# Backward chain cut into sixteen pieces of even TensorE work, and the value projection split around the row sums

## The chip, the cores and the metric

The kernel runs on one core of one Trainium2 chip. The time is the device time of one execution in microseconds (us). The engines are TensorE (PE; its weight loads are listed apart as PEld), VectorE (DVE), ScalarE (ACT), GpSimd (POOL) and SyncE (SP, which only issues transfers; POOL issues some too).

## The reference

The program computes a gated mix of two attention branches over one sequence of 2048 tokens of width 576, and all its gradients:

```
g = sigmoid((x * gate_w).sum(-1))
a = A(x)      # 32 query heads of 18, one shared key and value head, softmax, output projection
b = B(B_x)    # 64 segments of 32 tokens, 32 heads of 128; 8 memory rows stand before each segment
out = g * a + (1 - g) * b
grads = vjp(out)(grad_out)    # of x, wq, wk, wv, wo, mem0, Wq, Wk, Wv, Wo, gate_w
```

In branch B the first eight rows of a segment's output are the memory of the next segment:

```
for s in range(64):
    h = concatenate([mem, xs]); q, k, v = h @ Wq, h @ Wk, h @ Wv     # per head
    o = softmax(mask(q k^T * scale)) v;  o = sum over heads of o @ Wo
    mem = o[:, :8];  outs.append(o[:, 8:])
```

So the forward pass of the memory rows is a chain of 64 dependent segments, and their gradient is a chain of 64 in reverse order. All other work can be done in bulk.

## The kernel before

The memory rows are handled in two chains, `b_chain_fwd` and `b_chain_bwd`. Both are generators: each `yield` ends a piece, and there are sixteen pieces to a segment. Each chain is woven with a sweep of branch A, which is bulk work: `a_pass1` with the forward chain, `a_pass2` with the backward chain. A sweep has 1024 steps and 64 segments have 1024 pieces, so one piece stands against one step. `weave` runs under a manual schedule: what is written first is issued first, on every engine and every queue. The order on TensorE is piece, step, piece, step.

A step n of the backward sweep `a_pass2` issues two matmuls into `b_S` (scores of step n+1), two into two tiles of `b_dP` (step n), one exponential on ScalarE (`b_S` to `b_E`, L1532), two products on VectorE (`b_dP` times `b_E` to `b_dS`, L1553), and four matmuls into `b_acc` (step n-1). `b_S` has one buffer, and `b_dP` has two, one for each of the two tiles, so each waits for the reader of the step before. The forward sweep has the same form with `a_S`, `a_dP`, `a_E`, `a_W` (L1394, L1424), and eight matmuls into `a_acc`. Every fourth step issues two loads on SP (`b_QD`, `b_SD`), eight steps ahead of their use.

A backward segment, by its sixteen pieces (0 to 15):

- 0 to 3: gradient of the segment's memory rows times Wo^T, in two column halves j (tile `r_pj`, 20 matmuls each, five weight blocks of 128 rows, called kts); 12 matmuls, then 8 and a copy to `r_dOm` on ScalarE, twice.
- 4: transpose to `r_dOT` (ScalarE) and the product `r_prod` (VectorE). 5: dP in `r_x`, then `r_dS` (VectorE) and its spread form `r_dSB` (POOL).
- 6, 8, 10: `mem_grad` for v, k and q: 16 matmuls with a full 128x128 array, and a copy to `r_dT` on ScalarE. Piece 6 also has `r_dspad` and `r_dsq` on VectorE. Piece 10 also issues the store of `r_dT` (`dTm_dram`, POOL) and the 14 loads of the next segment (`load`, SP).
- 7, 9, 11 to 14: `heads(wi, hf)`, the gradient times Wv, Wq and Wk (wi 2, 0, 1), in two column halves hf of 288: 32 matmuls each, eight units u of four matmuls side by side. After (1, hf) ScalarE copies the half to `r_hs`. Piece 11 also has `r_xq`: two copies on POOL (`r_xpad`, L828), a transpose on VectorE (L830), four stores on POOL (`pq_dram`, L932). Piece 14 also has `sums` of the first two blocks and `p_blocks` for the next segment (`r_ppad` on POOL, `r_pq` on VectorE, `r_PqB` on POOL).
- 15: the other sums, and the copy to `dm`, which the next segment's piece 0 reads.

In a forward segment, pieces 6 to 9 are: value projection of half 0 (20 matmuls into `c_pj`), scores and exponential (`c_E`), the row sums (two matmuls into `c_x`, L66, and the reciprocal `c_rd`, L359), and value projection of half 1 with the copy `c_v` (L63), the normalised `c_pn` (L365) and its spread form `c_PB` (POOL). Piece 11 (`po`) multiplies `c_PB` by the values.

Of the kernel before, what the change touches and what calls it, by code (L numbers as in the profile page):

```python
# [10 lines left out]
F32 = mybir.dt.float32  # L11
P = 128
# [18 lines left out]
class Kern:  # L31
# [205 lines left out]
    def b_chain_fwd(self, keep, sp, psum):  # L237
        nc = self.nc
        NSEG = self.NSEG
# [47 lines left out]
        for s in range(NSEG):  # L287
            h_ = hm[s % 2]
            nc.gpsimd.dma_start(self.memT_dram[:, :, s, :], h_[:, :, 0:8])
            t2 = {w: sp.tile([P, 8, E], BF16, name=f"c_{w}2", bufs=1) for w in ("k", "q", "v")}  # L290
# [20 lines left out]
            def proj(w, j):  # L311
                pj = self.proj_mem(h_, self.W[w], j, psum, "c_pj", 1)
                self.evac(flat(t2[w], j), pj[:], use="s")
# [38 lines left out]
            Et = sp.tile([P, 2, 64], BF16, name="c_E", bufs=1)  # L352
            nc.scalar.activation(Et[:].rearrange("p a b -> p (a b)"), ps[:], ACT.Exp, scale=SCALEB)
            yield
            den = psum.tile([P, 64], F32, name="c_x", bufs=1)
            self.mm(den[:], lhsT=self.blockones[:], rhs=Et[:, 0, :], start=True, stop=False)
            self.mm(den[:], lhsT=self.blockones[:], rhs=Et[:, 1, :], start=False, stop=True)
            rd = sp.tile([P, 64], F32, name="c_rd", bufs=1)
            nc.vector.reciprocal(rd[:], den[:])  # L359
            yield  # L360
            proj("v", 1)
            if s + 1 < NSEG:
                kx = load_k(s + 1)
            pn = sp.tile([P, 2, 64], BF16, name="c_pn", bufs=1)
# [21 lines left out]
            if s + 1 < NSEG:  # L386
# [21 lines left out]
                hs = None  # L408
                pm = None
                for lo, hi in ((0, 256), (256, 512), (512, 576), (576, 576)):  # L410
                    if hi > lo:
                        ph = half(lo, hi)
                    if lo:
                        kts = range(lo // P - 2, min(lo // P, NKT)) if lo < 576 else (4,)
# [5 lines left out]
                    if hi > lo:  # L420
                        hs = sp.tile([P, 256], F32, name="c_hs", bufs=1)
# [371 lines left out]
    def b_chain_bwd(self, keep, sp, psum):  # L793
        nc = self.nc
        NSEG = self.NSEG
# [37 lines left out]
        def p_blocks(pT):  # L833
            pq = to_q((pT[:, 1, :],), "p", nc.gpsimd)
            B = sp.tile([P, 8, 4, 8], BF16, name="r_PqB", bufs=1)
            self.expand(B[:], pq[:, 0, :, 0:8], 8)
            return B

        nxt = load(NSEG - 1)
        PqB = p_blocks(nxt["pT"])  # L840
        for s in reversed(range(NSEG)):
            L = nxt
            d_ = dm[s % 2]
            pT = L["pT"]
            nc.gpsimd.dma_start(self.dmT_dram[:, :, s, :], d_[:, :, 0:8])
            dOm = sp.tile([P, 8, E], BF16, name="r_dOm", bufs=1)
            for j in range(2):
                pj = psum.tile([P, 512], F32, name="r_pj", bufs=2)
                for kts in ((0, 1, 2), (3, 4)):
                    self.proj_part(pj, d_, self.WoT, j, kts)  # L850
                    if s == NSEG - 1 and j == 0 and kts[0] == 3:
                        self.load_WT()
                    if kts[0] == 3:
                        self.evac(dOm[:, 4 * j:4 * j + 4, :].rearrange("p u e -> p (u e)"), pj[:], use="s")
                    yield
            src = self.mem_T(dOm, psum, "r_x", 1)
            dOT = sp.tile([P, 8, 4, 8], BF16, name="r_dOT", bufs=1)
            nc.scalar.copy(dOT[:], src)
            prod = sp.tile([P, 8, 4, 8], BF16, name="r_prod", bufs=1)
            nc.vector.tensor_tensor(out=prod[:].rearrange("p u c q -> p (u c q)"),  # L860
                                    in0=dOT[:].rearrange("p u c q -> p (u c q)"), in1=L["oT"][:], op=ALU.mult)
            for c in range(4):
                nc.gpsimd.dma_start(self.mtok["dO"][s * 8:(s + 1) * 8, c * 1024:(c + 1) * 1024], self.m_rows(dOm, c))
            yield
            pd = psum.tile([P, 2, 64], F32, name="r_x", bufs=1)
            self.mm(pd[:].rearrange("p a b -> p (a b)"), lhsT=self.zeros[:], rhs=self.zeros[:], start=True, stop=False)
            for u in range(8):
                for c in range(4):
                    self.mm(pd[32 * c:32 * c + 32, 0, 8 * u:8 * u + 8], lhsT=L["vxT"][:, 8 * c + u, :],
                            rhs=dOT[:, u, c, :], start=False, stop=False, tp=(0, 32 * c))  # L870
            for u in range(8):
                for c in range(4):
                    self.mm(pd[32 * c:32 * c + 8, 1, 8 * u:8 * u + 8], lhsT=L["vmT"][:, 8 * c + u, :],
                            rhs=dOT[:, u, c, :], start=False, stop=False, tp=(0, 32 * c))
            for rg in range(2):
                for c in range(4):
                    self.mm(pd[32 * c:32 * c + 32, rg, :], lhsT=self.negones[:, 0:32], rhs=prod[:, :, c, :],
                            start=False, stop=True, tp=(0, 32 * c))
            dS = sp.tile([P, 2, 64], BF16, name="r_dS", bufs=1)
            nc.vector.scalar_tensor_tensor(out=dS[:], in0=pd[:], scalar=SCALEB, in1=pT[:], op0=ALU.mult, op1=ALU.mult)  # L880
            dSB = sp.tile([P, 16, 4, 8], BF16, name="r_dSB", bufs=1)
            self.expand(dSB[:], dS[:].rearrange("p a (u q) -> p (a u) q", q=8), 16)
            yield
            dT = sp.tile([P, 3, 8, 32], BF16, name="r_dT", bufs=1)
            hs = sp.tile([P, D], F32, name="r_hs", bufs=1)
            ph = {}

            def heads(wi, hf):
                if hf not in ph:
                    ph[hf] = psum.tile([P, 288], F32, name="r_pj", bufs=2)  # L890
                for u in range(8):
                    for g in range(4):
                        self.mm(ph[hf][32 * g:32 * g + 32, :], lhsT=dT[:, wi, u, :],
                                rhs=self.WT[wi][:, 8 * g + u, 288 * hf:288 * hf + 288],
                                start=(wi == 2 and u == 0), stop=(wi == 1 and u == 7), tp=(0, 32 * g))
                if wi == 1:
                    nc.scalar.copy(hs[:, 288 * hf:288 * hf + 288], ph[hf][:])

            def sums(kts):
                for kt in kts:  # L900
                    ncols = KT_ROWS[kt]
                    self.mm(pm[0:ncols, kt, :], lhsT=hs[:, kt * P:kt * P + ncols], rhs=self.selF[:, :])

            def mem_grad(wi, name, pairs):
                pg = psum.tile([P, 8, 32], F32, name=name, bufs=2 if name == "r_pj" else 1)
                for u in range(8):
                    for n, (l, r) in enumerate(pairs):
                        self.mm(pg[:, u, :], lhsT=l[u], rhs=r[u], start=(n == 0), stop=(n == 1))
                nc.scalar.copy(dT[:, wi], pg[:])

            rows = lambda t, lo=0: [t[:, u, lo:lo + E] for u in range(8)]
            blk = lambda t, u0=0: [f(t[:, u0 + u]) for u in range(8)]
            mem_grad(2, "r_pj", ((rows(mrow["dx"], E), [seln] * 8), (rows(dOm), blk(PqB))))
            dSq = to_q((dS[:, 1, :],), "ds", nc.vector)
            yield
            heads(2, 0)
            yield
            mem_grad(0, "r_x", ((rows(L["kx"]), blk(dSB)), (rows(mrow["k"]), blk(dSB, 8))))
            dSqB = sp.tile([P, 8, 4, 8], BF16, name="r_dSqB", bufs=1)
            self.expand(dSqB[:], dSq[:, 0, :, 0:8], 8)  # L920
            yield
            heads(2, 1)
            yield
            mem_grad(1, "r_x", ((rows(mrow["dx"]), [seln] * 8), (rows(mrow["q"]), blk(dSqB))))
            nc.gpsimd.dma_start(self.dTm_dram[s // 16][:, :, s % 16, :], dT[:].rearrange("p w u c -> p w (u c)"))
            if s:
                nxt = load(s - 1)
            yield
            heads(0, 0)
            xq = to_q((pT[:, 0, :], dS[:, 0, :]), "x", nc.gpsimd)  # L930
            for c in range(4):
                nc.gpsimd.dma_start(self.pq_dram[s // 4, s % 4, :, c, :, 32 * (s % 4):32 * (s % 4) + 32],  # L932
                                    xq[32 * c:32 * c + 8].rearrange("p i u k -> p (i u) k"))
            yield
            heads(0, 1)
            yield
            heads(1, 0)
            yield
            heads(1, 1)
            pm = psum.tile([P, NKT, 8], F32, name="r_x", bufs=1)  # L940
            sums((0, 1))
            if s:
                PqB = p_blocks(nxt["pT"])
            yield
            sums((2, 3, 4))
            dn = dm[1 - s % 2]
            nc.vector.tensor_copy(dn[:, 0:4, 0:8], pm[:, 0:4, :])
            nc.vector.tensor_copy(dn[0:64, 4, 0:8], pm[0:64, 4, :])
            yield
# [849 lines left out]
```

## Time and profile before

| what | value |
|---|---|
| median of 3 runs | 6491.99 us (6484.06 to 6493.47) |
| the profiled execution | 6472.94 us, span of its core 6471.1 us, mean granted TensorE clock 0.971 |
| PE busy | 5931.5 us, 92% of the span |
| DVE, ACT, POOL busy | 3769.7 (58%), 3481.2 (54%), 1952.8 us (30%) |
| forward weave | from about 507 to 2436 us |
| backward weave | from about 3251 to 5039 us |

A busy share is an average over the whole span. The times of the two weaves are those of their first and last exponential in the timeline. A wait in the profile names the engine or transfer that came last; PE's matmuls are pipelined, so start times show more than ends.

### The profile page before, as it was taken

To read this page: it belongs to the slowest core of one execution; us is meant where nothing else is said; L and a number is where in the kernel's file an instruction comes from. 1 tells how busy PE (TensorE), PEld (TensorE's weight loads), DVE (VectorE), ACT (ScalarE), POOL (GpSimd) and SP (SyncE) were. 2 spreads that over 40 slices of the span, in tenths; PEclk is the share of its full clock that TensorE was granted. 3 is DMA by queue.
4 is the path that set the end of the run, shared out by engine and by line. 5 is a ranking of instruction groups with operands and counts; after the bars stand their busy time and mean duration, and the time that the engine had idled before them with its cause. 6 is when DMAs were issued, how large, how long until landed. Compare 5 with 4: busy or idle time off the path is not lost. (4 is left out here: it accounts for less than half of the span.)

```text
span 6471.1 us, 208564 instructions
## 1 busy us (share of the span) xinstructions
PE 5931.5 (92%) x88611; PEld 3332.0 (51%) x88822; DVE 3769.7 (58%) x7061; ACT 3481.2 (54%) x5105; POOL 1952.8 (30%) x3451
## 2 busy tenths in 40 slices
PE   7898999999999995999879999999999899899997
PEld 5443444444444443778634444444444677675443
DVE  5336777777777773666568888888887211111111
ACT  3326777777777773656556767667776322211100
POOL 3002333333333333444423333333333111112212
PEclk9998999999999997999989999999999899999998
DMA  4636666666664435999854443333434799896643
GB/s 152 225 145 114 115 120 119 120 117 118 120 118 104 98 79 167 252 253 263 251 184 101 103 102 102 97 100 102 102 102 100 201 247 245 232 275 213 216 146 111
DMA packets 1368108, 991.94 MB, mean 153 GB/s; under 512 B 931613, under 2 KB 1184806, under 8 KB 1356486
## 3 DMA queue, kind: packets, MB, share of 16 engines
q1 hardware_dynamic: 1285030, 780.53, 49.3%
q0 software_dynamic: 82144, 198.05, 9.6%
q8 instruction: 696, 11.40, 0.7%
q14 instruction: 238, 1.95, 0.1%
HBM read 552.41 MB, written 384.76 MB: 145 GB/s over the span
## 5 line engine op out<-in xcount | busy, mean ns | idle before, releaser
L1424 DVE TENSOR_TENSOR a_W<-a_dP,a_E 128x512 bf16<-128x512 f32 x2048 | 1314.8, 684 | 478.9 <-PE a_dP L66 377.0
L1553 DVE TENSOR_TENSOR b_dS<-b_dP,b_E 128x512 bf16<-128x512 f32 x2048 | 1315.8, 684 | 328.0 <-PE b_dP L66 245.4
L1532 ACT ACTIVATE b_E<-b_S 128x1024 bf16<-128x1024 f32 x1024 | 1048.9, 1024 | 529.2 <-PE b_dP L66 393.6
L1394 ACT ACTIVATE a_E<-a_S 128x1024 bf16<-128x1024 f32 x1024 | 1052.1, 1027 | 134.5 <-PE a_dP L66 120.9
L66 PE MATMUL b_dP<-b_KV,b_QD 32*128 32x512 bf16 x2048 | 584.9, 382 | 5.2 <-DVE b_dS L1553 5.2
L66 PE MATMUL b_S<-b_KV,b_QD 32*128 32x512 bf16 x2048 | 401.6, 385 | 128.9 <-ACT b_E L1532 82.4
L66 PE MATMUL a_dP<-a_QD,l_KV 32*128 32x512 bf16 x2048 | 513.3, 382 | 1.0 <-DVE a_W L1424 0.8
L66 PE MATMUL w_acc<-w_d,w_h 128*128 128x512 bf16 (+1 forms) x2352 | 470.9, 379 | 2.5
L66 PE MATMUL a_S<-a_QD,l_KV 32*128 32x512 bf16 x2048 | 399.6, 383 | 74.3 <-ACT a_E L1394 72.4
L66 PE MATMUL r_pj<-WT,r_dT 128*32 128x288 bf16 x12288 | 447.0, 288 | 0.0
L66 PE MATMUL a_acc<-a_W,l_WK 128*32 128x512 bf16 x4096 | 410.5, 390 | 0.1
L66 PE MATMUL b_acc<-b_dS,b_SD 128*32 128x512 bf16 x2048 | 406.0, 393 | 0.0
L66 PE MATMUL b_acc<-b_E,b_SD 128*32 128x512 bf16 x2048 | 405.8, 393 | 0.0
L66 PE MATMUL a_acc<-a_E,l_VK 128*32 128x512 bf16 x4096 | 399.9, 380 | 0.0
L66 PEld LDWEIGHTS <-r_dT 128*32 128x32 bf16 x12288 | 330.6, 97 | 78.9 <-issue 1.1
L1027 DVE COPY y_T<-y_pt 128x512 bf16<-128x512 bf16 x256 | 96.8, 419 | 461.1 <-PE y_pt L71 443.6
L66 PEld LDWEIGHTS <-w_h 128*128 128x128 bf16 (+1 forms) x2400 | 213.1, 100 | 244.5 <-issue 3.4
L66 PEld LDWEIGHTS <-hm 128*32 128x32 bf16 x7680 | 207.0, 97 | 229.2 <-issue 15.0
L66 PEld LDWEIGHTS <-b_SD 128*32 128x32 bf16 x4096 | 105.3, 93 | 421.3 <-issue 420.3
L66 PEld LDWEIGHTS <-b_QD 32*128 32x128 bf16 x4096 | 142.9, 91 | 327.2 <-issue 245.3
L66 PEld LDWEIGHTS <-l_WK 128*32 128x32 bf16 x4096 | 105.3, 93 | 349.0 <-issue 348.9
L1013 ACT CAST y_tdk<-y_pk 128x512 bf16<-128x512 f32 x128 | 75.1, 587 | 379.9 <-PE y_pk L66 240.8
(410 smaller groups left out, 11558.8 us busy)
## 6 DMA issues: line engine op xcount, KB each, us to landing
b_QD<-qd_dram SPq DMA_DIRECT2D x256, 128.0 KB
b_SD<-sd_dram SPq DMA_DIRECT2D x256, 128.0 KB
dOx_dram<-p_tok SPq DMA_DIRECT2D x16, 1024.0 KB
c_vx<-vx_dram SPq DMA_DIRECT2D x256, 64.0 KB
krow_dram<-c_k POOLq DMA_DIRECT2D x64, 256.0 KB, 2.6
qrow_dram<-c_q POOLq DMA_DIRECT2D x64, 256.0 KB, 2.8
vrow_dram<-c_v POOLq DMA_DIRECT2D x64, 256.0 KB, 4.5
x_q<-qx_dram SPq DMA_DIRECT2D x32, 512.0 KB
```

The costliest lines, as they stand in the source:

```text
L66: return self.nc.tensor.matmul(out, lhsT, rhs, start=start, stop=stop, tile_position=tp, skip_group_check=True)
L1013: nc.scalar.copy(d[w][:, r, :], pk[:])
L1027: nc.vector.tensor_copy(T_[t][w][:], pt[:])
L1394: nc.scalar.activation(E_[n][:], S.pop(n)[:], ACT.Exp, scale=SCALEA)
L1424: nc.vector.tensor_tensor(out=W_[n][:, i, :], in0=dP[i][:], in1=E_[n][:, i, :], op=ALU.mult)
L1532: nc.scalar.activation(E_[n][:], S.pop(n)[:], ACT.Exp, scale=SCALEA)
L1553: nc.vector.tensor_tensor(out=D_[n][:, i, :], in0=dP[i][:], in1=E_[n][:, i, :], op=ALU.mult)
```

## The change

The forward chain issues 12 of the 20 matmuls of the second half of the value projection in the piece of the row sums' place, ahead of them, and the row sums, their reciprocal, the last 8 matmuls and the rest of the old projection piece in the next one. The backward chain's Wo^T projection takes three pieces instead of four (16, 12 and 12 matmuls), across the border of the column halves. The 48 units of `heads` are taken from one list, six or three at a time, so that a piece may end in the middle of a weight or of a column half: six in each pure piece, three behind the second and third `mem_grad`. Both chains still have sixteen pieces to a segment. In the new numbering a backward segment has the projection in 0 to 2, `r_dOT` in 3, dP in 4, `mem_grad` in 5, 7 and 9, units in 6 to 14, `r_xq` in 11, the copy of the first half of `r_hs` in 12, `p_blocks` in 13, the first sums in 14, the others in 15. The same instructions are issued, in another order.

```diff
@@ b_chain_fwd
             nc.scalar.activation(Et[:].rearrange("p a b -> p (a b)"), ps[:], ACT.Exp, scale=SCALEB)
             yield
+            pj = psum.tile([P, 512], F32, name="c_pj", bufs=1)
+            self.proj_part(pj, h_, self.W["v"], 1, (0, 1, 2))
+            yield
             den = psum.tile([P, 64], F32, name="c_x", bufs=1)
...
             nc.vector.reciprocal(rd[:], den[:])
-            yield
-            proj("v", 1)
+            self.proj_part(pj, h_, self.W["v"], 1, (3, 4))
+            self.evac(flat(t2["v"], 1), pj[:], use="s")
@@ b_chain_bwd
-            for j in range(2):
-                pj = psum.tile([P, 512], F32, name="r_pj", bufs=2)
-                for kts in ((0, 1, 2), (3, 4)):
-                    self.proj_part(pj, d_, self.WoT, j, kts)
...
-                    yield
+            pj = [psum.tile([P, 512], F32, name="r_pj", bufs=2) for _ in range(2)]
+            for k, parts in enumerate((((0, (0, 1, 2, 3)),), ((0, (4,)), (1, (0, 1))), ((1, (2, 3, 4)),))):
+                for j, kts in parts:
+                    self.proj_part(pj[j], d_, self.WoT, j, kts)
+                    if kts[-1] == 4:
+                        self.evac(dOm[:, 4 * j:4 * j + 4, :].rearrange("p u e -> p (u e)"), pj[j][:], use="s")
...
+                yield
...
-            def heads(wi, hf):
...
+            units = iter([(wi, hf, u) for wi, hf in ((2, 0), (2, 1), (0, 0), (1, 0), (0, 1), (1, 1)) for u in range(8)])
+
+            def heads(n):
+                for _ in range(n):
+                    wi, hf, u = next(units)
...
             yield
-            heads(2, 0)
+            heads(6)
             yield
             mem_grad(0, "r_x", ((rows(L["kx"]), blk(dSB)), (rows(mrow["k"]), blk(dSB, 8))))
...
-            yield
-            heads(2, 1)
+            heads(3)
+            yield
+            heads(6)
             yield
             mem_grad(1, "r_x", ((rows(mrow["dx"]), [seln] * 8), (rows(mrow["q"]), blk(dSqB))))
...
-            yield
-            heads(0, 0)
+            heads(3)
+            yield
+            heads(6)
+            yield
+            heads(6)
             xq = to_q((pT[:, 0, :], dS[:, 0, :]), "x", nc.gpsimd)
...
             yield
-            heads(0, 1)
-            yield
-            heads(1, 0)
-            yield
-            heads(1, 1)
+            heads(6)
+            yield
+            heads(6)
+            if s:
+                PqB = p_blocks(nxt["pT"])
+            yield
+            heads(6)
             pm = psum.tile([P, NKT, 8], F32, name="r_x", bufs=1)
             sums((0, 1))
-            if s:
-                PqB = p_blocks(nxt["pT"])
             yield
             sums((2, 3, 4))
```

More of the change, by code (lines that the diff above doesn't have):

```diff
@@ L846, in b_chain_bwd @@
             dOm = sp.tile([P, 8, E], BF16, name="r_dOm", bufs=1)
-            for j in range(2):
-                pj = psum.tile([P, 512], F32, name="r_pj", bufs=2)
-                for kts in ((0, 1, 2), (3, 4)):
-                    self.proj_part(pj, d_, self.WoT, j, kts)
[L851 to L854, printed above, removed]
-                    yield
+            pj = [psum.tile([P, 512], F32, name="r_pj", bufs=2) for _ in range(2)]
[4 more added lines that the diff above has]
+                        self.evac(dOm[:, 4 * j:4 * j + 4, :].rearrange("p u e -> p (u e)"), pj[j][:], use="s")
+                if s == NSEG - 1 and k == 1:
+                    self.load_WT()
+                yield
             src = self.mem_T(dOm, psum, "r_x", 1)
@@ L886, in b_chain_bwd @@
             ph = {}
-            def heads(wi, hf):
-                if hf not in ph:
-                    ph[hf] = psum.tile([P, 288], F32, name="r_pj", bufs=2)
-                for u in range(8):
+            units = iter([(wi, hf, u) for wi, hf in ((2, 0), (2, 1), (0, 0), (1, 0), (0, 1), (1, 1)) for u in range(8)])
+            def heads(n):
+                for _ in range(n):
+                    wi, hf, u = next(units)
+                    if hf not in ph:
+                        ph[hf] = psum.tile([P, 288], F32, name="r_pj", bufs=2)
                     for g in range(4):
@@ L895, in heads @@
                                 start=(wi == 2 and u == 0), stop=(wi == 1 and u == 7), tp=(0, 32 * g))
-                if wi == 1:
-                    nc.scalar.copy(hs[:, 288 * hf:288 * hf + 288], ph[hf][:])
+                    if wi == 1 and u == 7:
+                        nc.scalar.copy(hs[:, 288 * hf:288 * hf + 288], ph[hf][:])
             def sums(kts):
```

## The prediction

> **What bounds the kernel now.** The change touches only the two stages in which a chain is woven with a sweep, so I first ask for the windows of these stages (start, length, then busy PE, PEld, DVE, ACT, POOL, granted clock, DMA share):
> ```profile
> 552.00:2408.00 1856.00, 1783.48 (x32841) 821.74 (x32838) 1377.62 (x2465) 1374.48 (x1907) 666.70 (x1359) 1.00 0.57 112
> 3330.00:4992.00 1662.00, 1565.91 (x30067) 773.12 (x30066) 1365.68 (x2414) 1164.19 (x1452) 552.68 (x965) 1.00 0.40 101
> ```
> No engine is full: PE 96% forward, 94% backward, DVE 74 and 82%. So I look for a loop between engines. The waits of the backward stage (total us, times, longest):
> ```profile
> ACT b_E L1532 <- PE b_dP L66: 390.9, 507, 22.0
> DVE b_dS L1553 <- PE b_dP L66: 233.9, 514, 21.5
> PE b_S L66 <- ACT b_E L1532: 80.5, 313, 0.6
> ```
> Each waits for another in turn. The timeline of two successive backward rounds shows how (start, us, what):
> ```profile
> 3980.20 0.39 PE L66 MATMUL b_S<-b_KV,b_QD 32*128 32x512 bf16 x2 [0.33 <-ACT b_E L1532]
> 3980.21 0.68 PE L66 MATMUL b_dP<-b_KV,b_QD 32*128 32x512 bf16 x2
> 3980.68 1.02 ACT L1532 ACTIVATE b_E<-b_S 128x1024 bf16<-128x1024 f32 x1 [0.26 <-ACT r_dT L909]
> 3980.73 1.29 DVE L1553 TENSOR_TENSOR b_dS<-b_dP,b_E 128x512 bf16<-128x512 f32 x2 [0.26 <-PE b_dP L66]
> 3980.82 0.39 PE L66 MATMUL b_acc<-b_dS,b_SD 128*32 128x512 bf16 x2
> ...
> 3981.05 1.15 PE L66 MATMUL r_pj<-WT,r_dT 128*32 128x288 bf16 x32
> ...
> 3982.14 0.39 PE L66 MATMUL b_S<-b_KV,b_QD 32*128 32x512 bf16 x2
> ...
> 3982.46 0.39 PE L66 MATMUL b_acc<-b_dS,b_SD 128*32 128x512 bf16 x2
> ...
> 3982.69 1.16 PE L66 MATMUL r_pj<-WT,r_dT 128*32 128x288 bf16 x32
> ```
> A round runs from one b_S to the next. Two rules follow. (1) b_S has one buffer: 0.47 us to the exponential, 1.02 of it, 0.06 to the next b_S, so no round is under 1.55. (2) The DVE pair starts 0.53 after b_S and ends 1.29 later; the second b_dP of the next round waits for it, and the b_acc behind it starts 2.17 us after the earlier b_S (or 0.33 after its own). So a round is the larger of 1.55 and max(0.33, 2.17 - previous round) + 0.23 (b_acc) + w, where w is the piece's time on PE. Here 32 head matmuls (w 1.09) follow a 1.55 round: 0.62 + 0.23 + 1.09 = 1.94, as seen; the next head piece costs 0.33 + 0.23 + 1.08 = 1.64, as seen (3982.14 to 3983.78). A piece with w under 0.70 is free, and one over it is dearer behind a short round than behind a long one. That is what a rearrangement can win or lose.
>
> **Backward, part by part.** From the starts of the exponentials in the segment at 3962.50 the sixteen rounds are 1.60, 1.55, 1.61, 1.55 (projection), 1.55, 1.78 (dOT, dP), 1.55, 1.94, 1.55, 1.94, 1.55 (gradients and heads), 1.94, 1.64, 1.85 (heads), 2.18, 1.55 (heads and sums): 27.33 us. Put through the rules with w 0.75 for 12 projection matmuls, 0.50 for 8, 0.40, 0.93, 0.53 for mem_grad, 1.08 for heads, 0.54 and 0.90 for sums, they give 27.28, so the rules hold to 0.05.
>
> Nothing is added or removed; 48 head units (0.135 each: 1.08/8) and 20 projection steps move. Changed pieces, by the rules:
> - 0: 16 matmuls, w 0.75 + 0.22: 0.62 + 0.23 + 0.97 = 1.82. 1: w 0.75 behind a long round, 1.55. 2: 0.62 + 0.23 + 0.75 = 1.60.
> - 3 (dOT): the ScalarE copy of piece 2's projection (0.56) now starts only when 12 matmuls are done (1.70), ends at 2.26, and the exponential due at 2.07 is 0.19 late: 1.74. In the old order it lay behind 8 matmuls and just fitted.
> - 4 (dP): 0.43 + 0.23 + 0.93 = 1.59, against 1.78, because a long round precedes. 5: 1.55. These six rounds take 9.85; seven took 11.19, and the heads now have ten rounds instead of nine.
> - 6: six units, w 0.81: 1.66, and 0.02 for dS on DVE. 7: mem_grad and three units, w 0.94; the two DVE operations for dSq (0.49 between pairs) hold that pair by 0.25, which a 1.94 round covered before: 0.74 + 0.23 + 0.94 = 1.91. 8: 1.55. 9: 0.62 + 0.23 + 0.94 = 1.78. 10: 1.55. 11: 1.66. 12: 1.55.
> - 13: r_xq (0.61 on DVE, issued in piece 11) delays the pair by 0.24: 0.86 + 0.23 + 0.81 = 1.90. 14: 0.33 + 0.23 + 0.81 + 0.54 = 1.91. 15: 1.55.
>
> Sum 26.89: 0.39 below the rules' own 27.28, 0.44 below the measured 27.33; I take 0.41. The gain is small although PE work is even, since a six-unit piece is still over 0.70.
>
> Moved with the pieces: dTm's issue (0.76 on POOL) and the fourteen loads of the next segment come one piece earlier. On SP the loads stay in the same place among the b_QD/b_SD loads and their wait (r_dx, for the third mem_grad) ends one round sooner: no cost. On POOL, dTm and the two r_xpad copies now have two rounds before r_xq wants them instead of one. In five rows of r_xq, DVE waits for r_xpad (7.4 us in total); where dTm is 1.65 late, round 13 takes 1.48 more: 7 us that go. p_blocks also comes a piece earlier, two rounds after r_xq instead of three: its r_ppad copy sits on POOL behind four pq_dram issues (0.61 each) and ends 2.96 after r_xq. DVE would stop 0.36 for it, which the 1.91 round of piece 14 covers (free up to 3.3). Five other segments show 4.2: about 0.9 each, 5 us. Net 2 us won.
>
> **Forward.** The timeline of a segment around the row sums:
> ```profile
> 1190.53 0.23 PE L66 MATMUL c_x<-c_E,blockones 128*128 128x64 bf16 x2
> ...
> 1191.04 0.39 PE L66 MATMUL a_S<-a_QD,l_KV 32*128 32x512 bf16 x2 [0.28 <-ACT a_E L1394]
> ...
> 1191.23 0.55 DVE L359 RECIPROCAL c_rd<-c_x 128x64 f32<-128x64 f32 x1
> ...
> 1192.11 1.25 PE L66 MATMUL c_pj<-Wv,hm 128*32 128x512 bf16 x20
> ...
> 1192.83 0.46 DVE L365 TENSOR_TENSOR c_pn<-c_E,c_rd 128x128 bf16<-128x128 bf16 x1
> ...
> 1193.41 0.59 ACT L63 CAST c_v<-c_pj 128x512 bf16<-128x512 f32 x1 [0.87 <-PE c_pj L66]
> ```
> The row-sum piece leaves PE idle 0.28 before a_S; the 20 matmuls behind it (1.18 to the next a_S at 1193.29) make a round of 2.25. With 12 of them ahead, the first a_S comes at 1191.14 (0.10 later). The next piece is the sums (about 0.2) and 8 matmuls (0.5), and its a_S comes at 1192.82, 0.47 earlier; but c_rd and c_pn, which stood on both sides of a DVE pair, now stand back to back between two (about 0.85), the pair is 0.47 late, and by the po piece only 0.07 is left of the gain. In the half-projections the round is no longer held by DVE, and 0.27 remains. I take 0.25 a segment; if c_pn must wait out c_rd's full 0.55 it is 0.1, if DVE hides it 0.5.
>
> **A rule against it.** A switch of the tile shape in the array is dear if it idles PE: the change adds two such switches per backward segment (mem_grad to heads) and one forward. The rows: 32 loads of heads take 1.06 and the next shape starts 1.09 after the first head, so 0.03; a switch to 128*128 shows 0.10 (3979.20 to 3979.30), which w 0.53 holds. Three at 0.03 to 0.10 are 6 to 19 us over 63 segments; I take 6. [...]
>
> **Sum.** Backward 0.41 x 63 = 26, POOL 2, forward 0.25 x 63 = 16, switches -6: 38 us off. The first backward segment (51 us, heads waiting for WT) keeps its transfer, so it is not counted. The profiled execution took 6472.9 (span 6471.1): 6435. The median shown is 6492.0, 19 above; I carry the difference over: 6454.
>
> **Rivals.**
> - No change (15%): 0.2% is 13 us, about what a measurement tells from none. If the 0.10 switch price, 0.1 forward and no POOL gain hold: 26 + 6 - 19 = 13, 6479. For it: the rounds' gains and losses (-1.34 in the first block, +0.90 in the heads) nearly cancel.
> - A large gain (10%): if evenly filled rounds settle at (2.40 + 0.81)/2 = 1.61, a segment is 25.8, and 1.5 x 63 + 16 gives 6381. Against it: DVE's extra operations sit in rounds 6 and 12.
> - Slower (10%): POOL to DVE. If r_ppad comes 4.2 or more after r_xq in every segment, DVE stops 1.6 in round 14 and 0.9 is left: 57 us lost and, with switches at 0.10, 19 more; 26 + 16 + 7 won: +27, 6519. It decides from a lag of 3.3. Against it: 58 of 63 rows show 2.96.
> - My forecast (65%): 6454.
>
> The range: 0.25 us a segment backward either way (16 us) for the rules' error, and the ends of the forward and switch prices. Low: 42 + 2 + 32 - 6 = 70 off, 6422, taken to 6410 toward the large gain. High: 10 + 2 + 6 - 19, so 6493, taken as 6495; it holds the no-change case.
>
> **What would show it.** Right: backward segments near 26.9, rounds as listed, the exponential 0.19 late in round 3, r_xpad waits gone; forward segments near 29.75 (30.02 before), c_rd and c_pn adjacent. Wrong: backward segments of 27.3 or more, or r_pq waiting over 1 us for r_ppad.

## The result and the profile after

| | before | after |
|---|---|---|
| median, runs side by side | 6489.53 us (4 runs) | 6495.08 us (4 runs) |
| ratio of the times | | 1.0007, 95% interval [0.9989, 1.0024] |
| the profiled execution | 6472.94 us, span 6471.1 | 6496.09 us, span 6494.3 |
| forward stage, first to last exponential | 1928.0 us | 1959.1 us |
| backward stage, the same | 1787.0 us | 1775.1 us |
| median forward segment | 30.02 us | 30.21 us |
| median backward segment | 27.33 us | 27.16 us |

The change makes no difference that can be measured. The forecast was 6454 us, with a range of 6410 to 6495; the median lies 0.08 above its upper end. In the profiled executions the backward stage gave 12 us, the forward stage lost 31, and the rest of the program differs by 4: 23 us in all, of which the medians show 6.

The windows of the two stages in the profile after (start and end, length, then busy PE, PEld, DVE, ACT, POOL, granted clock, DMA share, GB/s):

```profile
554.00:2440.00 1886.00, 1820.57 (x32851) 818.46 (x32839) 1409.74 (x2467) 1374.68 (x1907) 667.65 (x1361) 0.99 0.59 111
3360.00:5010.00 1650.00, 1585.03 (x30020) 756.22 (x30018) 1356.99 (x2409) 1165.12 (x1450) 552.76 (x963) 0.99 0.39 101
```

About as many matmuls as before take 37 us longer on PE in the forward window (1783 before), and DVE is 32 us busier with the same work: something made instructions longer, not only waits. The granted clock is 0.99, where it was 1.00.

The waits of the backward stage (engine and tile waiting, releaser: total us, times, longest):

```profile
ACT b_E L1542 <- PE b_dP L66: 381.3, 581, 19.5
DVE b_dS L1563 <- PE b_dP L66: 273.8, 634, 19.6
PE b_S L66 <- ACT b_E L1542: 47.0, 174, 0.5
DVE r_pq L833 <- POOL r_ppad L831: 28.4, 60, 1.6
ACT b_E L1542 <- ACT r_dT L915: 16.9, 62, 0.5
```

The loop is the one of before, with less of PE waiting for the exponential (47 us instead of 80). New is r_pq waiting for r_ppad, 0.37 us in the median, as worked out (0.36) and covered; the waits for r_xpad (7.4 us) are gone.

Now the rounds (start to start of the exponentials), as medians over the segments. Backward:

| round | 0 | 1 | 2 | 3 | 4 | 5 | 6 | 7 | 8 | 9 | 10 | 11 | 12 | 13 | 14 | 15 | sum |
|---|---|---|---|---|---|---|---|---|---|---|---|---|---|---|---|---|---|
| predicted | 1.82 | 1.55 | 1.60 | 1.74 | 1.59 | 1.55 | 1.68 | 1.91 | 1.55 | 1.78 | 1.55 | 1.66 | 1.55 | 1.90 | 1.91 | 1.55 | 26.89 |
| measured | 1.82 | 1.55 | 1.73 | 1.56 | 1.66 | 1.55 | 1.69 | 1.99 | 1.55 | 1.94 | 1.55 | 1.69 | 1.55 | 1.79 | 2.00 | 1.55 | 27.16 |

Forward, the six rounds that changed (the others are the same to 0.01):

| round | 8 | 9 | 10 | 11 | 12 | 13 | sum |
|---|---|---|---|---|---|---|---|
| before | 1.55 | 2.38 | 1.56 | 1.55 | 2.05 | 2.24 | 11.33 |
| after | 1.69 | 1.87 | 2.09 | 1.76 | 1.75 | 2.34 | 11.50 |

The 0.5 us won in round 9 is lost again in round 10. The timeline of a forward segment after shows where (start, us, engine, line, what):

```profile
1202.22 0.23 PE L66 MATMUL c_x<-c_E,blockones 128*128 128x64 bf16 x2
...
1202.93 0.55 DVE L362 RECIPROCAL c_rd<-c_x 128x64 f32<-128x64 f32 x1
...
1203.11 1.05 POOL L1504 TENSOR_TENSOR a_qt<-a_qt,a_rl 128x512 bf16<-128x512 bf16 x1
...
1203.57 0.74 DVE L368 TENSOR_TENSOR c_pn<-c_E,c_rd 128x128 bf16<-128x128 bf16 x1
...
1204.23 2.50 DVE L1434 TENSOR_TENSOR a_W<-a_dP,a_E 128x512 bf16<-128x512 f32 x4
...
1205.56 0.37 PE L66 MATMUL a_dP<-a_QD,l_KV 32*128 32x512 bf16 x1 [0.23 <-DVE a_W L1434]
```

c_pn, 0.46 us before, takes 0.74 and ends at 1204.31, 0.15 after POOL's a_qt (1204.16). The pair a_W behind it starts late, the next a_dP waits for a_W, and so does the exponential. The same rows in the profile before, with POOL's instruction ahead of a_qt:

```profile
1192.71 0.43 POOL L1492 TENSOR_TENSOR a_dq<-a_t,a_rl 128x144 bf16<-128x144 f32 x1
1192.83 0.46 DVE L365 TENSOR_TENSOR c_pn<-c_E,c_rd 128x128 bf16<-128x128 bf16 x1
1193.10 1.10 POOL L1494 TENSOR_TENSOR a_qt<-a_qt,a_rl 128x512 bf16<-128x512 bf16 x1
```

There c_pn started before a_qt, but beside a_dq, which ends at 1193.14; c_pn ends at 1193.29, again 0.15 later. In 61 of the 64 segments before, c_pn ends 0.14 to 0.15 after a_dq, so 0.46 was already a held duration. No wait is listed, so a reader of waits alone sees nothing: the hold lies inside the instruction's own duration.

The second loss is the clock. Four windows around one place of the forward stage after (columns as above):

```profile
868.00:870.50 2.50, 2.27 (x36) 0.90 (x37) 2.21 (x5) 1.02 (x1) 2.30 (x4) 1.00 0.44 86
870.50:873.00 2.50, 2.50 (x44) 1.41 (x37) 1.38 (x3) 1.02 (x1) 0.94 (x2) 0.51 0.88 204
873.00:875.00 2.00, 2.00 (x48) 1.05 (x44) 1.28 (x2) 1.40 (x2) 0.00 (x0) 0.76 0.85 294
875.00:877.00 2.00, 2.00 (x58) 1.40 (x51) 0.98 (x4) 1.17 (x2) 0.00 (x0) 1.00 0.82 115
```

In the second the granted clock is 0.51, and the timeline there shows 32 projection matmuls taking 1.94 us. In the segment shown above the same 32 take 1.05:

```profile
871.10 1.94 PE L66 MATMUL c_pj<-WoN,c_oT 128*32 128x256 bf16 x32
...
1207.67 1.05 PE L66 MATMUL c_pj<-WoN,c_oT 128*32 128x256 bf16 x32
```

By the trace's clock record the forward stage after has 12 such stretches of 3.41 us at half clock and one of 6.8 at its very end, the one before 1 (of 6.8 us). Ten of the 12 make round 12 take 3.1 to 3.4 us instead of 1.75; one lengthens rounds 11 and 12, one round 0. Each costs 1.3 to 1.7 us, the 12 together 17.

So the 31 us of the forward stage divide like this: 63 segments x 0.19 = 12 us from the median round, 17 us from the rise of the mean over the median (30.17 - 30.02 before, 30.63 - 30.21 after, times 63), and 2 us in the last rounds. Of these 17, 15 are the half-clock stretches: 17 us after, less 2.4 for the one before.

### The profile page after: what moved, and what is told of

Read it like the earlier page. It is cut to its first block, busy times and chain, and to the rows that moved or that the text cites. A ratio compares the mean times of both kernels' runs of the same rounds, so it can differ in the third digit from the quotient of the medians.

```text
span 6494.3 us, 208624 instructions
## 1 busy us (share of the span) xinstructions
PE 5991.1 (92%) x88611; PEld 3310.1 (51%) x88822; DVE 3794.4 (58%) x7061; ACT 3484.4 (54%) x5105; POOL 1955.4 (30%) x3451
## 4 chain that ended last, share of the span: by engine, by line
PE 41%; issue 6%; ACT 6%; DMA 5%; SPq 2%; POOL 1%; DVE 1%; POOLq 0%; DVEq 0%; ACTq 0%
PE w_acc L66 10%; PE r_pj L66 6%; ACT b_E L1542 5%; PE b_S L66 5%; PE b_acc L66 4%; PE r_x L66 3%; PE b_dP L66 3%; DMA dsx_dram<-x_dS 3%; PE x_tr L71 2%; PE y_pdx L66 2%; PE x_po L66 1%; PE x_b L66 1%; PE f_big L66 1%; PE x_m L66 1%; PE x_S L66 1%
## 5 line engine op out<-in xcount | busy, mean ns | idle before, releaser
L66 PE MATMUL r_pj<-WT,r_dT 128*32 128x288 bf16 x12288 | 480.6, 288 | 1.2 <-DMA WT<-st_WT 1.2
L66 PEld LDWEIGHTS <-r_dT 128*32 128x32 bf16 x12288 | 317.6, 97 | 84.9 <-issue 2.2
```

The lines of the kernel that those rows point to most:

```text
L66: return self.nc.tensor.matmul(out, lhsT, rhs, start=start, stop=stop, tile_position=tp, skip_group_check=True)
```

## The experiments

Each stage is judged by its own segments, so that forward and backward can be edited apart in one kernel.

**The two halves of the change.** First the kernel before once more, to see whether half-clock stretches are its own:

> The kernel before, unchanged, profiled a second time. Theory (the half-clock windows of the forward weave come from the new order): 0 to 2 windows of half clock between the first and the last forward exponential, a forward weave of 1925 to 1935 us, a median forward segment of 30.02 and a median backward segment of 27.33. Rival (the windows come by chance from run to run): 6 or more, and a forward weave of 1940 or more.

Measured: forward segment 30.03 us, stage 1927.9, no stretch at half clock; backward 27.34 and 1785.0.

Then the backward part alone and the forward part alone (all hunks of one generator, none of the other):

> The backward chain of the change with the forward chain of before. Theory (the backward part gains a little, since TensorE pays about 0.14 us for each mem_grad-to-heads switch): median backward segment 27.16, backward weave near 1775, forward weave 1928, some 12 us less than before: 6478, ratio 0.998. Rival (the parts disturb each other, or the backward part is itself the loss): no gain, 6490 or more.

> The forward chain of the change with the backward chain of before. Theory (reciprocal and c_pn back to back hold VectorE by 1.2 us and, besides, half-clock windows appear): median forward segment 30.21, forward weave 1945 to 1960 with 8 or more half-clock windows, backward weave as before; 6505 to 6520, ratio 1.003 to 1.005. Rival (the forward part alone is neutral and the loss needs both parts): 6490, no windows.

| run | time, ratio to before (6473.57, 24 runs beside them) | forward segment, stage, half-clock stretches | backward segment, stage |
|---|---|---|---|
| backward alone | 6467.38, 0.9988 [0.9979, 0.9998] | 30.03, 1929.5, 1 | 27.17, 1774.4 |
| forward alone | 6485.50, 1.0017 [1.0006, 1.0027] | 30.20, 1943.3, 7 | 27.34, 1788.9 |

What follows: the parts are independent. The backward part is a small gain (6.2 us, 0.1%, its interval just below 1), the forward part a small loss (11.9 us) with many half-clock stretches. Their sum, 5.7 us lost, is what both together showed (5.6), too little to tell from none there.

**Is it the two DVE operations standing together?** The reciprocal moved one piece ahead of c_pn:

```diff
+            den = ...; mm(den, blockones, Et) x2; rd = reciprocal(den)
             pj = psum.tile([P, 512], F32, name="c_pj", bufs=1)
             self.proj_part(pj, h_, self.W["v"], 1, (0, 1, 2))
             yield
-            den = ...; mm(den, blockones, Et) x2; rd = reciprocal(den)
             self.proj_part(pj, h_, self.W["v"], 1, (3, 4))
```

> As the run before it in this list, but the row sums and the reciprocal stand ahead of the 12 matmuls in their piece, and c_pn stays with the 8 matmuls in the next, so that a pair of sweep products lies between the two VectorE operations again. Theory (adjacency on VectorE is the forward loss): median forward segment 29.65, 0.55 less than with the two adjacent; forward weave near 1905 if no half-clock window comes, 1920 with ten of them; 6468 to 6483. Rival (the early 12 matmuls themselves are the loss, since they starve the later pieces): segment 30.1 or more.

Measured: 6494.11 us, ratio 1.0033 [1.0023, 1.0043]; forward segment 30.21, stage 1958.4, 20 half-clock stretches. My theory that the adjacency costs the time fell. The timeline of this run says why:

```profile
1200.63 1.05 POOL L1497 TENSOR_TENSOR a_qt<-a_qt,a_rl 128x512 bf16<-128x512 bf16 x1
1200.72 1.11 DVE L368 TENSOR_TENSOR c_pn<-c_E,c_rd 128x128 bf16<-128x128 bf16 x1
```

c_pn started earlier, nearly together with a_qt, and took 1.11 us: it again ended 0.15 after a_qt. So not the place of c_pn in DVE's order counts, but the end of what POOL runs beside it. That made the theory for the next runs.

**A common base without the transposing loads.** From here on all kernels use plain loads in place of the transposing ones:

> The kernel before, with every transposing DMA load (368 of them, of keys, values and gradients) replaced by a plain load of the same bytes: the values land in other places, so the transposition of these operands is left out of the computation; all instructions of the engines stay. It is the base for the three runs beside it, which leave out the same. Both theories: the rounds of the two woven stages do not hang on these loads, so the forward segment is 30.0 and the backward one 27.3, as in the kernel before, with at most a few half-clock stretches; the whole time is the same or some per cent less, in the sweeps outside these stages.

> The changed kernel with plain loads in place of the transposing ones, as in the base beside it. Forward segment 30.2, with c_pn at 0.7 us or more ending when POOL's a_qt ends, and 5 or more half-clock stretches; backward segment 27.16 with rounds 7 and 9 at 1.99 and 1.94. If the forward loss hung on the transposing loads it would be under 29.9.

Measured: 6399.5 us for the base, with forward 30.03 and 1923.5 (1 stretch), backward 27.34 and 1785.9; 6411.3 us for the changed kernel, with forward 30.21 and 1943.2 (7 stretches), backward 27.17 and 1774.5. c_pn takes 0.74 and ends 0.15 after a_qt. The base is some 90 us faster than the full kernel before, and the two stages have under 6 us of that; in them all median rounds are those of the full kernels, to 0.01, so what these kernels show of the rounds can be carried to the full ones.

**POOL out of the way; units ahead of mem_grad.**

```diff
-            if post is not None and n % 16 in (1, 4, 6):
+            if post is not None and n % 16 in (1, 4, 5):
...
+            heads(3)
             mem_grad(0, ...)     # and the same ahead of mem_grad(1, ...)
...
-            heads(3)
```

> The changed kernel (plain loads as in the base) with two edits, one in each stage. Forward: POOL's after-segment work, which ends in a_qt (1.05 us), is called behind step 5 of a segment, not step 6, so that it ends about 2 us earlier. Theory (DVE's c_pn is held off while a_qt runs): c_pn 0.46 again, segment about 29.7, 0 to 2 half-clock stretches, stage 1905 to 1915 us. Rival (the order itself is longer): segment still 30.1 or more. Backward: in the two pieces of a mem_grad and three head units the units stand first, one change of tile shape fewer each. Theory (mem_grad to heads costs about 0.14 us, not 0.03): round 9 about 1.80 instead of 1.94, round 7 about 1.85 instead of 1.99, segment about 26.95. Rival (the DVE operations or the units set them): rounds 7 and 9 as before, segment 27.1 to 27.2.

Measured: 6355.9 us. Forward segment 29.76, no stretch at half clock, stage 1904.1. c_pn takes 0.29 and round 10 falls from 2.09 to 1.64; the five other changed rounds stay as they were, to 0.01. The timeline of this run:

```profile
1148.67 1.05 POOL L1506 TENSOR_TENSOR a_qt<-a_qt,a_rl 128x512 bf16<-128x512 bf16 x1
...
1150.62 0.55 DVE L364 RECIPROCAL c_rd<-c_x 128x64 f32<-128x64 f32 x1
...
1151.26 0.29 DVE L370 TENSOR_TENSOR c_pn<-c_E,c_rd 128x128 bf16<-128x128 bf16 x1
...
1151.47 1.28 DVE L1436 TENSOR_TENSOR a_W<-a_dP,a_E 128x512 bf16<-128x512 f32 x2
```

a_qt is done 1.5 us before c_pn starts, and the pair a_W follows at once. One number moved in one line of another loop, and the forward part of the change gains what the prediction gave it: 30.02 - 29.76 = 0.26 us a segment (0.25 predicted). The call that moved holds all of POOL's after-segment work, a_dq too, so c_pn stands clear of both. The hold is shown as the cause of the longer median round.

Backward: segment 26.95 as expected. Round 9 fell from 1.94 to 1.83, round 7 from 1.99 to 1.87. PE's rows of round 9, first after and then in this run, show what one change of tile shape costs:

```profile
4004.49 0.39 PE L66 MATMUL b_acc<-b_dS,b_SD 128*32 128x512 bf16 x2
...
4004.82 0.19 PE L66 MATMUL r_x<-seln,r_dx 128*128 128x32 bf16 x1
...
4005.32 0.55 PE L66 MATMUL r_pj<-WT,r_dT 128*32 128x288 bf16 x12
...
4005.80 0.39 PE L66 MATMUL b_S<-b_KV,b_QD 32*128 32x512 bf16 x2
```
```profile
3895.44 0.39 PE L66 MATMUL b_acc<-b_dS,b_SD 128*32 128x512 bf16 x2
...
3895.67 0.54 PE L66 MATMUL r_pj<-WT,r_dT 128*32 128x288 bf16 x12
3896.14 0.19 PE L66 MATMUL r_x<-seln,r_dx 128*128 128x32 bf16 x1
...
3896.64 0.39 PE L66 MATMUL b_S<-b_KV,b_QD 32*128 32x512 bf16 x2
```

From b_acc to the next shape it is 0.33 where the shape changes (`128*32` to `128*128`) and 0.23 where it doesn't; the whole stretch from b_acc to b_S is 1.31 with three changes and 1.20 with two. One change costs about 0.11 us here.

**Other edits of both chains.** The sums first and the early POOL call together, and DVE's work moved in the backward chain:

```diff
-            dSq = to_q((dS[:, 1, :],), "ds", nc.vector)      # behind mem_grad(2, ...)
...
+            dSq = to_q((dS[:, 1, :],), "ds", nc.vector)      # behind mem_grad(0, ...)
...
+            xq = to_q(..., "x", nc.gpsimd) and its four stores      # from piece 11 to piece 9
```

> The changed kernel (plain loads as in the base) with other edits. Forward: the row sums and the reciprocal ahead of the 12 projection matmuls, and the early POOL call too. Theory (a_qt holds c_pn): c_pn falls from 1.11 to about 0.46, segment 29.7 or less, at most 2 half-clock stretches. Rival: 30.1 or more, 10 or more stretches. Backward: DVE's copy and transposition for dSq issued behind the second mem_grad piece instead of the first, and the r_xq transposition with its stores two pieces earlier. Theory (a DVE operation costs most behind a long round's neighbour with much PE work): by the rules 0.25 to 0.5 less a segment, 26.7 to 26.9. Rival: DVE's work only moves its delay to another round, or POOL's queue is late for r_pq: 27.1 or more.

Measured: 6345.2 us. Forward segment 29.62, no stretch at half clock, stage 1895.1, c_pn 0.28 instead of 1.11: the order that lost the most with the hold is the best one without it. Backward 26.98 (expected 26.7 to 26.9): rounds 7 and 13 fell to 1.80 and 1.69, but round 14 rose from 2.00 to 2.10. A gain of 0.19 instead of 0.25 or more, part of the delay only moved.

**Control: the early POOL call in the old order.** One line, as above, in the base:

> Control: the kernel before (plain loads as in the base) with POOL's after-segment work called behind step 5 instead of step 6. Theory: in the old order c_pn ended 0.9 us before a_qt did and was held only a little (0.46 instead of the 0.29 it takes when POOL is quiet), with no wait behind it, so nothing is won: forward segment 30.0 (29.9 to 30.1), stage about 1924, 0 or 1 half-clock stretch. Rival (an early POOL call shortens any order, so the collision is not the cause): 29.8 or less.

Measured: 6396.4 us, forward segment 30.03, stage 1920.9, no stretch. c_pn falls from 0.46 to 0.28 here too, and no round changes: in the old order c_pn stood ahead of a DVE pair that waited for PE anyway (0.54 us in the profile before). The early call is worth something only to the new order.

**Are the half-clock stretches a matter of how busy TensorE is?** Three matmuls more, in a gap of PE behind the hold:

```diff
             src = self.mem_T(t2["v"], psum, "c_pj", 1)
+            fl = psum.tile([P, 256], F32, name="c_x", bufs=1)
+            for _ in range(3):
+                self.mm(fl[:], lhsT=self.blockones[:], rhs=self.W["v"][:, 0, 0:256])
```

> The changed kernel (plain loads as in the base) with three matmuls of 256 columns whose result nobody reads (about 0.32 us) behind the transposition of the memory values, where TensorE waits 0.33 us for the next a_S. Theory (the half-clock stretches come because TensorE is busy for too little of a stretch of about 3.4 us around the c_pn hold): 0 to 2 stretches in the forward stage instead of 7 to 13, although the median segment does not fall (30.2, at most 30.3) and c_pn still takes 0.74; the stage 1930 to 1937 us instead of 1943 to 1959. Rival (the stretches come of something else in the new order, such as DVE's or POOL's load or the number of shape changes): 5 or more stretches.

Measured: 6396.8 us against 6411.3 without them. One stretch (6.8 us long) in the forward stage instead of 7; median segment 30.20 and c_pn 0.74, unchanged; stage 1935.7 instead of 1943.2. Work that nobody reads made the stage shorter; two runs of the base differ by 3.4. It is one run, and the number of stretches differs from run to run (12, 7 and 7 in the three runs of the new order without the filler, 0 to 2 in the six of the old one), but it is outside both the expectation of the rival (5 or more) and all runs of its own order. It supports, without settling it, that the stretches follow the gaps in PE that the hold makes; the runs without the hold, which have none (0 in each of the two above), point the same way.

**All edits together, timed beside the base.** The edits of the two combined runs in one kernel:

> The changed kernel (plain loads in place of the transposing ones, as in the base) with all edits that shortened a stage: row sums and reciprocal ahead of the 12 matmuls, the early POOL call, head units ahead of mem_grad in the mixed pieces, DVE's work for dSq and r_xq moved. If the edits add up: forward segment 29.62 as with the first two alone; backward round 9 at 1.83 instead of 1.94 and round 7 at about 1.70 instead of 1.80, so 26.77 instead of 26.98, stage about 1742 us; the whole about 6335 us against about 6400 of the base timed beside it, a ratio near 0.99. Rival (removing one hold uncovers another in the backward chain): 26.9 or more.

> The base (the kernel before with plain loads in place of the transposing ones) once more, timed, so that the run beside it can be compared with it: about 6400 us, forward segment 30.03, backward 27.34.

Measured: 6334.15 us (4 runs), 0.9752 [0.9737, 0.9767] of the full kernel before; the base 6400.33 us (4 runs), 0.9856 [0.984, 0.9872] of the same. The intervals do not meet; the edits are worth 66 us, 1.0%, over the base. Forward 29.61 and 1894.7, backward 26.81 (26.77 expected) and 1743.6. Against the base of this pair the forward stage gives 32 us and the backward stage 38. These edits were not run in a kernel with the transposing loads; that they would win the same there is inferred from the rounds, which do not hang on the loads, and was not measured.

## Why the prediction was wrong

The forecast had three terms of weight, and the step that failed is the forward one: c_rd and c_pn back to back at "about 0.85", which took 1.38. Timed apart, the forward part lost 12 us where 16 were to be won, and the backward part with its switches won 6 where 24 were.

- **Forward, 0.25 x 63 = 16 us won.** Measured: 31 us lost in the profiled execution, 15 in that of the forward part alone. Without the hold c_rd and c_pn take 0.93 (1150.62 to 1151.55), and then the gain is 0.26, as predicted; the steps come out too (0.37 us early behind the 8 matmuls where 0.47 was forecast, 0.08 by the po piece where 0.07 was). With the hold they take 1.38 (1202.93 to 1204.31), and 0.45 us are lost in round 10. I took c_pn's duration as its own. In its old place it was already held, by the end of a_dq, and in its new place a_qt (1.05 us, 0.43 for a_dq) runs beside it. The row of a_qt stood 0.27 us behind c_pn in the same timeline, and that of a_dq 0.12 ahead; I asked of POOL only what waits for it, not what it does beside. The bound "if c_pn must wait out c_rd's full 0.55 it is 0.1" had no case for a longer c_pn. Its condition held (c_pn starts 0.64 behind c_rd in both runs) and did not decide, since c_pn alone takes 0.29 and not 0.46: that 0.26 meets 0.25 so closely is in part luck. The hold did not fall on all of DVE's work: c_pn takes 0.29 us alone, 0.74 and 1.11 beside a_qt, while c_rd, most of it beside the same a_qt, stays at 0.55, and a pair a_W beside a_qt (at 1149.41 in the run with the early call) takes 1.29, as elsewhere. c_pn has both inputs in SBUF, while c_rd and the a_W products read PSUM for one; they differ in size and type too, and which of these decides no run shows.
- **Not in the sum at all: the clock.** Half-clock stretches cost about 17 us of the profiled execution. The granted clock of the forward window before was 1.00, and I took it as given. With the longer hold it fell 7 to 20 times in a forward stage (once with the filler), without it not once in three runs.
- **Switches, 6 us.** A switch costs PE time, as I had taken it (0.33 us from b_acc to the next shape, 0.23 without a switch), and the size was off. I took 0.03 each and kept 0.10 as the bound. Measured 0.11 and 0.12 for the two backward ones: 0.23 x 63 = 14 us instead of 4; the forward one was not measured apart. The 0.10 of the row was the right price, and spoke against the change with reason.
- **Backward, 26 us won.** Rounds 0, 1, 5, 6, 8, 10, 12 and 15 came to within 0.01, and 3 with 2 together to 0.05 (the late copy of piece 2's projection falls on round 2 in the median, not 3). Of the 0.27 us by which the sum of the rounds is short (the switches stood outside it), rounds 7 and 9 are 0.24, together the price of the two switches (0.23), though not round by round (0.08 and 0.16); rounds 4, 11 and 14 took 0.19 more and 13 came 0.11 better, not explained one by one. 12 us were won in the stage of the profiled execution.
- **POOL, 2 us.** Right in kind: r_xpad's waits are gone, r_pq waits 0.37 in the median and 1.5 to 1.6 in five segments, near the 0.36 and 1.6 worked out. The 2 us themselves cannot be told from the rest. The slower rival (POOL late for r_pq in every segment) did not come true.

The no-change rival came true, at 15%, and for half of its reasons: its switch price of 0.10 is near the measured one, but it took the forward part as a small gain. That the forward loss and the backward gain nearly cancel is luck.

## What to carry to other kernels

Before a DVE operation is moved, look at what POOL runs in its new place, not only at who waits for whom: c_pn took 0.29 us alone and 0.74 beside POOL's a_qt, and this hold appeared in no list of waits. When an instruction's duration differs between two traces, look for the one on another engine with which it ends. When a reordering loses, find the one collision before giving up the order: here one step number elsewhere turned the forward part from a loss of 0.19 us a segment to a gain of 0.26.

## What the runs showed of the hardware that I had not expected

- A 128x128 bf16 multiplication on DVE that takes 0.29 us alone was stretched to 0.74 and 1.11 by a 128x512 one on POOL of 1.05 us; in the changed kernel it ended 0.15 after POOL's in 63 of 64 segments (the first has no a_qt beside it). In the kernel before a shorter one on POOL (a_dq, 0.43 us) stretched it to 0.46 in the same way. POOL's a_qt took 1.05 in the first cases and 1.10 in the kernel before, where it starts while c_pn still runs.
- TensorE's clock was halved for 3.41 us at a time with no gap in PE of that length: the waits listed behind the hold are 0.33 and 0.23 us, and in the 3.41 us ahead of eleven of the 12 stretches after, PE's rows leave no gap over 0.41 (ahead of the one at 785.20, 1.41). The clock record gives 3.413 us for each of the 12, and in this trace the starts of all of them lie whole multiples of that length apart. Some come 92.16 us apart (870.53, 962.69, 1054.85), which is 27 such lengths, and about three segments with one stretch's loss (3 x 30.21 + 1.4 = 92.0): so the sweep comes back to nearly the same place between the multiples.
- With three matmuls whose result is not read in such a gap, the forward stage was 7.5 us shorter (one run).
